# FFT mixing and a routed two-layer network: the transform's steps at other places of a block, outputs scaled a block later, four PSUM banks for the small blocks' second layer

## The chip, the core and the metric

The kernel runs on one core of a Trainium2 chip, as one program. The core's engines work side by side, each through its own queue in order: TensorE (PE: matmuls, with PEld for its weight loads), VectorE (DVE), ScalarE (ACT), GpSimd (POOL, which here also issues the row scatters) and SyncE (SP, which issues most loads and stores). Matmul results land in the banks of PSUM, from where VectorE and ScalarE read them. Semaphores hold an instruction back until what it needs is done.

The metric is the device time of one execution in microseconds. Before the change it is 1346.84, the median of 17 runs (1344.0 to 1351.41).

## The reference

```python
def _attn_ref(x):                      # x: 8 x 2496 x 256
    X = np.fft.fft(x, axis=1)
    X = np.fft.fft(X, axis=2)
    return X.real.astype(np.float32)

def _moe_ref(x, w_gate, w1, w2):       # x: 19968 x 256, 8 experts, F = 1024
    logits = x @ w_gate
    expert_idx = np.argmax(logits, axis=1)
    ...                                # probs: softmax of the logits
    gate_w = probs[np.arange(N), expert_idx]
    ...                                # rows sorted by expert; for expert e:
        h = np.maximum(x_sorted[lo:hi] @ w1[e], 0.0)
        y_sorted[lo:hi] = h @ w2[e]
    ...                                # rows back in place
    return (gate_w[:, None] * y).astype(np.float32)
```

Each of 8 batches of 2496 rows goes through a two-dimensional Fourier transform, of which the real part is kept; each resulting row goes to the one expert with the highest logit, through two matrix products with a ReLU between them, and is scaled by its softmax weight.

## The kernel before

**The transform** of a batch has two stages. `first(b)` folds the input on VectorE (L296 to L308), multiplies it on TensorE (`s`), and stores the result to DRAM as `Td` (L344); `regroup` (L353) loads it back in another order as `t`. `second(b)` (L363) rotates one column (`turn_last`: product `pr`, copy L374), multiplies groups (`group`: product `p` from `t`, copied to `zz` at L381), and for each of ten windows forms output rows and logits (product `p` from `zz`; copy L407; L410, L412; mirrored halves L386). After each five windows `route` (L418) finds the expert of each row by a chain of small VectorE operations (L426 to L433), counts rows before it by matmuls (`rk`), and fixes each row's place (L452 to L457). `send` (L464) then scatters 128 rows at a time into `Xs`, which holds the rows sorted by expert: ScalarE casts the places (`pi`, L469), GpSimd issues the scatter (L237).

**The plan.** When a batch is routed, `plan` (L478) decides which expert's rows each block of the next round takes: some 20 small VectorE operations, at whose end the table `p_tab` stands (L510, L511). SP reads the table into a register and loads a block's rows (`xb`, L530) and its expert's weights (`w1` at L537, `w2` at L539, 1 MB each). `fetch_some` (L783) does so up to three blocks ahead, in SP's queue order; rows only once all scatters of their batch are sent, and weights only once their table is made.

**The blocks.** Each round runs the blocks whose rows are there: rounds of batches 3 to 6 have five blocks of 512 rows, and the last has five of 512, seven of 256 and 21 of 128. A block's rows are transposed (`turn`: product `pt`, copy to `xT` at L579). From batch 3 on a 512-row block, and in the last round a 256-row block too, is computed with seven products in place of eight in each layer (Strassen's scheme in Winograd's form): sums of parts of the operands are formed first. The left operand's sums of layer one are made from w1 by `Left` (L544, VectorE, four steps at L558, into `ws`), during the block before. The right-hand sums come from `xT` (`right`, L563 to L566, VectorE). Layer one is `seven` (L608): 14 products into banks a, d, b, c, e, with sums on VectorE (L629) and copies and ReLUs on ScalarE (L694, L632). Bank b is used by two products, so the second waits until the first was read. Sums of the second layer's left operand stand between the layers: `ends` (L842, L843), `s2` (L890), `s4` (L894), on VectorE; its right operand's sums are `Below` (L588, L601), on GpSimd for 512-row blocks. Layer two is `lower` (L702): seven products into banks a, b and c, with sums into `y` (L726), scaling by the gate (`scaled`, L722, ScalarE) and the scatter of rows to the output (`send_rows`, GpSimd, L237).

**The order** is written out by hand. `experts` is a generator that yields after each product with a weight and a flag. The main loop (from L1014) runs it, and each yield whose flag is not `full` adds to `due`; for each whole unit of `due` one step of `side` is issued (L1030 to L1033). `side` for round b is `mixed(b)` (L954): stage two and routing of batch b woven with stage one of batch b + 1, then the plan. Scatters are issued by their own counter (`room`, L1037). So one engine's queue holds the instructions of the blocks and those of the transform in this written order, and an instruction that waits holds all behind it on its engine.

```python
            if not full:
                due += TICKS * w / ((SHARE if b >= LATE else EARLY) * open_) if w else 1
            while due >= 1:
                next(side, None)
```

## Time and profile before

| What | Value |
|---|---|
| median of 17 runs | 1346.84 us (1344.0 to 1351.41) |
| the profiled execution | 1346.9 us; its span, first to last instruction, 1345.1 us |
| mean granted clock of TensorE | 0.967 |
| busy: PE, DVE, ACT, POOL | 1254.8, 729.5, 504.6, 477.1 us |
| the chain that ended last | PE 77%, DVE 10%, issue 5%, DMA 4%, ACT 2%, POOL 2% |
| w1 and w2 loads, 1024 KB | 132, median 8.0 us from issue to landing |
| row scatters into Xs | 160, mean 1.04 us on POOL |

Rows of the profile name the line, the engine, the operation, and the tiles it writes and reads (out<-in). "x8" counts instructions; a bracket tells how long the engine stood idle before it and what ended this. Each 128x128 block of a matmul in fp32 appears as two records. Line numbers are those of the kernel the profile is of. Rounds of five 512-row blocks run from 346 to 990 us; before this the blocks are of other sizes and use eight products, and behind it the last round runs with no transform beside it.

### The profile page before, as it was taken

To read this page: it belongs to the slowest core of one execution; us is meant where nothing else is said; L and a number is where in the kernel's file an instruction comes from. 1 tells how busy PE (TensorE), PEld (TensorE's weight loads), DVE (VectorE), ACT (ScalarE), POOL (GpSimd) and SP (SyncE) were. 2 spreads that over 40 slices of the span, in tenths; PEclk is the share of its full clock that TensorE was granted. 3 is DMA by queue.
4 is the path that set the end of the run, shared out by engine and by line. 5 is a ranking of instruction groups with operands and counts; after the bars stand their busy time and mean duration, and the time that the engine had idled before them with its cause. 6 is when DMAs were issued, how large, how long until landed. Compare 5 with 4: busy or idle time off the path is not lost.

```text
span 1345.1 us, 23036 instructions
## 1 busy us (share of the span) xinstructions
PE 1254.8 (93%) x8191; PEld 1130.4 (84%) x8191; DVE 729.5 (54%) x1762; ACT 504.6 (38%) x1263; POOL 477.1 (35%) x435
## 2 busy tenths in 40 slices
PE   5769998999989999899999999999999999999997
PEld 3658987776889899898988989888989999999995
DVE  4643242242675756676666755677565663334451
ACT  1423242242345444454444434444433432222232
POOL 0336125034235633276333733275452421111112
PEclk7869999999999999999998999999999999999998
DMA  8877958437335523474332632243432347767675
GB/s 248 255 267 267 395 182 275 144 117 268 122 136 189 198 107 124 143 259 152 123 109 81 229 121 97 97 156 117 170 133 95 103 149 287 253 260 263 246 274 217
DMA packets 63119, 249.88 MB, mean 186 GB/s; under 512 B 10057, under 2 KB 24883, under 8 KB 43420
## 3 DMA queue, kind: packets, MB, share of 16 engines
q1 hardware_dynamic: 46231, 203.33, 43.7%
q0 software_dynamic: 15888, 42.14, 8.6%
q10 hardware_dynamic: 885, 2.94, 0.7%
q8 instruction: 66, 1.08, 0.3%
q14 instruction: 49, 0.40, 0.1%
HBM read 194.97 MB, written 54.83 MB: 186 GB/s over the span
## 4 chain that ended last, share of the span: by engine, by line
PE 77%; DVE 10%; issue 5%; DMA 4%; ACT 2%; POOL 2%; POOLq 0%; SPq 0%; DVEq 0%; ACTq 0%
PE a L222 20%; PE py L222 11%; PE c L222 11%; PE ph L222 11%; PE d L222 5%; PE b L222 5%; PE p L222 5%; PE e L222 3%; PE s L222 3%; PE pt L578 2%; DVE s L842 2%; DVE hT L843 1%; DMA xq<-in_x_dram 1%; DMA Td<-t 1%; DVE hT L629 1%
## 5 line engine op out<-in xcount | busy, mean ns | idle before, releaser
L237 POOL DMA_INDIRECT out_dram<-y,ro x163 | 165.1, 1013 | 600.6 <-ACT y L722 352.1
L237 POOL DMA_INDIRECT Xs<-rows,pi x160 | 166.9, 1043 | 257.4 <-ACT pi L469 155.4
L222 PE MATMUL ph<-xT,w_sb 128*128 128x128 f32 (+2 forms) x992 | 171.3, 329 | 0.8 <-ACT xT L579 0.8
L222 PE MATMUL py<-w_sb,hT 128*128 128x256 f32 x736 | 167.3, 382 | 0.0
L222 PEld LDWEIGHTS ph<-xT,w_sb 128*128 128x128 f32 x992 | 136.5, 193 | 24.8 <-issue 17.0
L222 PEld LDWEIGHTS py<-w_sb,hT 128*128 128x128 f32 x736 | 138.3, 192 | 17.7
L222 PE MATMUL a<-w_sb,hT 128*128 128x128 f32 x912 | 114.7, 278 | 3.3 <-ACT y L747 2.9
L222 PEld LDWEIGHTS a<-w_sb,hT 128*128 128x128 f32 x912 | 109.0, 192 | 10.1 <-ACT y L747 8.6
L859 DVE TENSOR_SCALAR hT<-ph 128x512 f32<-128x512 f32 x43 | 29.7, 690 | 159.9 <-PE ph L222 159.6
L632 ACT ACTIVATE hT<-hT 128x512 f32<-128x512 f32 x114 | 71.7, 631 | 93.3 <-DVE hT L629 93.1
L726 DVE TENSOR_TENSOR y<-y,c 128x256 f32<-128x256 f32 (+1 forms) x64 | 25.1, 392 | 139.9 <-ACT y L747 93.2
L579 ACT ACTIVATE xT<-pt,table 128x512 f32<-128x512 f32 (+1 forms) x94 | 59.2, 630 | 100.2 <-PE pt L578 98.4
L222 PE MATMUL a<-ws,hT 128*128 128x128 f32 x456 | 64.5, 299 | 11.0 <-DVE hT L890 10.9
L629 DVE TENSOR_TENSOR hT<-hT,c 128x512 f32<-128x512 f32 x57 | 39.2, 687 | 62.1 <-PE c L222 49.2
L911 ACT ACTIVATE y<-py,xb 128x256 f32<-128x256 f32 x49 | 23.2, 473 | 131.6 <-PE py L222 127.9
L222 PE MATMUL s<-xq,w 104*112 104x256 f32 (+2 forms) x208 | 61.2, 418 | 11.7 <-DVE xq L299 11.2
L601 POOL TENSOR_TENSOR ws<-w_sb,ws 128x512 f32<-128x512 f32 x50 | 70.7, 1413 | 2.8
L222 PEld LDWEIGHTS a<-ws,hT 128*128 128x128 f32 x456 | 59.9, 209 | 14.0 <-issue 10.4
L578 PE MATMUL pt<-table,xb 128*128 128x128 f32 x326 | 52.6, 278 | 15.6 <-DMA xb<-Xs 15.5
L722 ACT ACTIVATE y<-y,xb 128x128 f32<-128x128 f32 (+1 forms) x114 | 46.4, 449 | 51.8 <-DVE y L726 51.8
L410 DVE COPY lg<-p 128x16 f32<-128x16 f32 x80 | 13.8, 172 | 93.2 <-ACT zs L407 93.1
L222 PE MATMUL p<-table,t 120*128 120x120 f32 (+1 forms) x352 | 58.7, 293 | 4.9 <-ACT t L374 4.1
(162 smaller groups left out, 2570.2 us busy)
## 6 DMA issues: line engine op xcount, KB each, us to landing
w_sb<-in_moe_w_dram SPq DMA_DIRECT2D x132, 1024.0 KB, 8.0
xq<-in_x_dram SPq DMA_DIRECT2D x24, 896.0 KB, 9.0
xb<-Xs SPq DMA_DIRECT2D x28, 516.0 KB, 3.9
Td<-t SPq DMA_DIRECT2D x18, 448.0 KB, 3.3
t<-Td SPq DMA_DIRECT2D x8, 768.0 KB, 12.2
t<-Td SPq DMA_DIRECT2D x8, 640.0 KB, 13.9
xb<-Xs SPq DMA_DIRECT2D x13, 258.0 KB, 3.2
xb<-Xs SPq DMA_DIRECT2D x25, 129.0 KB, 3.3
```

The source lines that it names most:

```text
L222: nc.tensor.matmul(o, lhsT=lhsT, rhs=rhs, start=start, stop=stop, **kw)
L237: return unordered(pool.indirect_dma_start(out=dst, out_offset=bass.IndirectOffsetOnAxis(ap=idx, axis=0), in_=rows, in_offset=None, bounds ...
L578: nc.tensor.transpose(pt[:, c, t], xb[:, 2 * h + t, c * 128:(c + 1) * 128], ident[:])
L579: act.activation(xT[:, :, 256 * h:256 * h + 128 * n], pt[:].rearrange("p c t k -> p c (t k)"), ACTF.Copy, scale=con["alt"][:])
L601: self.eng.tensor_tensor(o, p, q, op=sub)
L629: vec.tensor_tensor(o, o, p[:], op=add)
L632: act.activation(o, o if p is None else p[:], ACTF.Relu)
L722: act.activation(y[k][:, i, lo:hi], y[k][:, i, lo:hi] if src is None else src[:, i], ACTF.Copy, scale=gate[:, k * nt + i])
L726: vec.tensor_tensor(o, o, p[:], op=add)
L842: vec.scalar_tensor_tensor(s1[:, at], h21[:, at], 0.0, h11[:, at], op0=ALU.max, op1=add)
L859: vec.tensor_scalar(o, ph[:], 0.0, None, op0=ALU.max)
L911: act.activation(y[:, i % 2], py[:], ACTF.Copy, scale=xb[:, i, D + 1:D + 2])
```

## The change

The yields of `seven` and `lower` now carry a second flag, so that steps of the transform are issued at three products of layer one (4 and 6) and behind the last four products of layer two only, and not between the layers' sums. Those of layer two weigh 1 and 4/3. A step of the transform may yield True (after the last window but one of the first half, and twice in routing); then no other step is issued at that place. `SHARE` goes from 0.6 to 0.9 and the open weight per block from 8 to 6.5, so the steps of a round are spread over more of it.

In `seven`, the sums of a half (`ends`) stand behind its last addition, and the weight sums (`step`) at other products. In `lower` for 512 rows the product 6 comes ahead of 5 and the transposes later; the second half of the output is scaled and sent by `rest`, which runs in the next block's layer one, ahead of the fourth of GpSimd's sums. For 256 rows `lower` is written anew with bank d, and in another order of products. The copy of the transposes moves from ScalarE to VectorE, but for the 512-row blocks with seven products. The number of matmuls stays the same.

```diff
--- before.py
+++ after.py
@@ -184,7 +184,7 @@
 
 TICKS = 32
 LATE = 4
-SHARE, EARLY, ROOM = 0.6, 0.7, 1.2
+SHARE, EARLY, ROOM = 0.9, 0.7, 1.2
 WARM = 16
 MOST = max(k for now in rounds() for _, k, _ in now)
 
@@ -411,7 +411,7 @@
                 for m, op in enumerate((ALU.add, ALU.subtract)):
                     vec.scalar_tensor_tensor(rows[:, k + m, 0:NY], p3[:, 0:NY], zs[:, 0:1], zs[:, 1:],
                                              op0=ALU.add, op1=op)
-                yield
+                yield w + 2 == HALF - 1
             mirror(rows, k)
             yield from route(b, h, rows, lg)
 
...
@@ -576,8 +576,11 @@
             for c in range(2):
                 for t in range(n):
                     nc.tensor.transpose(pt[:, c, t], xb[:, 2 * h + t, c * 128:(c + 1) * 128], ident[:])
-            act.activation(xT[:, :, 256 * h:256 * h + 128 * n], pt[:].rearrange("p c t k -> p c (t k)"), ACTF.Copy,
-                           scale=con["alt"][:])
+            o, i = xT[:, :, 256 * h:256 * h + 128 * n], pt[:].rearrange("p c t k -> p c (t k)")
+            if size == BIG and quartered(b, size):
+                act.activation(o, i, ACTF.Copy, scale=con["alt"][:])
+            else:
+                vec.tensor_scalar(o, i, con["alt"][:], None, op0=ALU.mult)
             yield xT
         if halved(b, size):
             th = size // 2
...
         a, b, c = [bank("a"), bank("d")], [None, None], [None, None]
         for k, g in ((0, 0), (0, 1), (1, 0), (5, 0), (5, 1), (1, 1), (4, 0), (4, 1), (6, 0), (6, 1), (2, 0), (3, 0),
@@ -684,22 +687,27 @@
                 product(g, 3, c[g], False)
                 plus(h21[g], c[g])
                 low(g)
-                if g:
-                    ends(0)
+                ends(g)
             else:
                 product(g, k, a[g], not k)
                 if k == 2:
                     relu(h12[g], a[g])
                 else:
                     act.copy({0: h11, 5: h21, 4: h22}[k][g], a[g][:])
-            if k in (0, 5):
+            if k == 0 or (k, g) in ((1, 1), (4, 0)):
                 step()
-            else:
+            if (k, g) == (4, 1):
+                step()
+                for f in later:
+                    f()
+                later.clear()
+            if k not in (0, 5):
                 sums()
-            yield
-        ends(1)
-
-    def lower(size, l, r, y, gate, send_rows, turn_some, s2, s4):
+            yield 4 <= k <= 6 and (k, g) not in ((5, 0), (5, 1), (6, 1))
+
+    later = []
+
+    def lower(size, l, r, y, gate, send_rows, turn_some, s2, s4, step):
 
 
 
@@ -726,38 +734,83 @@
             vec.tensor_tensor(o, o, p[:], op=add)
 
         a, b, c = (bank(k) for k in "abc")
+        if nt == 1:
+            d = bank("d")
+            p1, u2, u3 = y[1][:, 0:nt, 0:H], y[1][:, 0:nt, H:], y[0][:, 0:nt, 0:H]
+            high = y[0][:, 0:nt, H:]
+            product(0, a)
+            act.copy(p1, a[:])
+            s2()
+            turn_some()
+            yield False
+            product(3, b)
+            yield False
+            product(1, a, False)
+            s4()
+            step()
+            turn_some()
+            yield False
+            product(5, c)
+            vec.tensor_tensor(u2, p1, c[:], op=add)
+            scaled(1, 0, H, a)
+            yield False
+            product(6, d)
+            vec.tensor_tensor(u3, u2, d[:], op=add)
+            step()
+            turn_some()
+            yield False
+            c = bank("c")
+            product(4, c)
+            vec.tensor_tensor(high, u3, c[:], op=add)
+            plus(u3, b)
+            plus(u2, c)
+            scaled(0, 0, D)
+            send_rows(0)
+            step()
+            yield False
+            d = bank("d")
+            product(2, d)
+            plus(u2, d)
+            scaled(1, H, D)
+            send_rows(1)
+            step()
+            yield False
+            return
         p1, u2, v = y[1][:, 0:nt, 0:H], y[0][:, 0:nt, 0:H], y[0][:, 0:nt, H:]
         product(0, a)
         act.copy(p1, a[:])
         s2()
-        yield
+        yield False
         product(1, b)
         s4()
         plus(p1, b)
-        yield
-        turn_some()
-        yield
+        yield False
+        product(6, c)
+        yield False
         product(5, a, False)
         act.copy(u2, a[:])
         scaled(1, 0, H)
-        yield
-        product(6, c)
-        yield
+        turn_some()
+        yield 1
         product(4, a, False)
         act.copy(v, a[:])
         plus(v, c)
         turn_some()
-        yield
+        yield 4 / 3
         product(2, a, False)
         scaled(1, H, D, a)
         send_rows(1)
         turn_some()
-        yield
+        yield 4 / 3
         product(3, c, False)
         plus(u2, c)
-        scaled(0, 0, D)
-        send_rows(0)
-        yield
+
+        def rest():
+            scaled(0, 0, D)
+            send_rows(0)
+
+        later.append(rest)
+        yield 4 / 3
 
     def experts(todo):
 
@@ -797,6 +850,10 @@
 
         for k, (b, size, last, at) in enumerate(todo):
             n, m = size // 128, BIG // size
+            if not (size == BIG and halved(b, size)):
+                for f in later:
+                    f()
+                later.clear()
             if not k:
                 while todo[0][:3] not in tabs:
                     yield 0, False
@@ -843,10 +900,10 @@
                     vec.scalar_tensor_tensor(h21[:, at], h21[:, at], 0.0, h22[:, at], op0=ALU.max, op1=sub)
 
             if halved(b, size):
-                for _ in seven(size, left.all, xT, hT, both, sums, step, ends):
+                for open_ in seven(size, left.all, xT, hT, both, sums, step, ends):
                     if size != BIG:
                         sums()
-                    yield 0.5, True
+                    yield 0.5, not open_
             for f in range(0 if halved(b, size) else FC // m):
                 ph = pse.tile([128, m, size], F32, tag="ac"[f % 2], name="ph")
                 with needed(last, at, ph):
@@ -876,7 +933,7 @@
             if both:
                 y = [bp.tile([128, 2, D], F32, tag="y", name="y", bufs=3) for _ in range(2)]
 
-                def send_rows(k):
+                def send_rows(k, n=n, ro=ro, y=y):
                     for i in range(n // 2):
                         at = k * n // 2 + i
                         put_row(out, ro[:, at:at + 1], y[k][:, i], NT - 1, "out")
@@ -895,9 +952,10 @@
 
                 while below.due:
                     below.step()
-                for _ in lower(size, (h22, h12, h12, h11, s1, h22, h21), below.all, y, xb[:, :, D + 1:D + 2],
-                               send_rows, turn_some, s2, s4):
-                    yield 1, False
+                for open_ in lower(size, (h22, h12, h12, h11, s1, h22, h21), below.all, y, xb[:, :, D + 1:D + 2],
+                                   send_rows, turn_some, s2, s4,
+                                   left.step if follow and halved(*follow[:2]) else lambda: None):
+                    yield open_ or 1, not open_
             for i in range(0 if both else n):
                 xT = next(turned, xT)
                 py = pse.tile([128, D], F32, tag="bd"[i % 2], name="py")
...
@@ -929,10 +989,11 @@
         parts = list(parts)
         while parts:
             for p in list(parts):
-                if next(p, p) is p:
+                r = next(p, p)
+                if r is p:
                     parts.remove(p)
                 else:
-                    yield
+                    yield r
 
     def close(b):
 
@@ -957,10 +1018,10 @@
         for _ in range(3):
             next(one, None)
             yield
-        for k, _ in enumerate(two):
+        for k, r in enumerate(two):
             if k % 2:
                 next(one, None)
-            yield
+            yield r
         yield from woven(close(b), one)
         yield from through(b)
 
@@ -1018,7 +1079,7 @@
             side = woven(chain(close(0), through(0)), chain(early, side))
         blocks = [(size, k * size / BIG, halved(b - 1, size)) for size, k, _ in rounds()[b - 1]]
         total = sum(k * (15 if seven_ else 16) for _, k, seven_ in blocks)
-        open_ = sum(k * (8 if seven_ else 16) for _, k, seven_ in blocks)
+        open_ = sum(k * (6.5 if seven_ else 16) for _, k, seven_ in blocks)
         while done < total:
             w, full = next(work)
             done += w
@@ -1029,8 +1090,9 @@
                 whole.update(p[0] for p in tabs if p != "cnt")
             if not full:
                 due += TICKS * w / ((SHARE if b >= LATE else EARLY) * open_) if w else 1
-            while due >= 1:
-                next(side, None)
+            stay = False
+            while due >= 1 and not stay:
+                stay = next(side, None) and halved(b - 1, BIG)
                 due -= 1
                 if b < LATE or not w:
                     send()
```

The cut places hold the two `yield True` of `route`, the seven `yield False` of the small form of `seven`, and the last run of what waits in `later` at the end.

More of the change, by code (lines that the diff above doesn't have):

```diff
@@ L433, in route @@
         vec.tensor_tensor(oh[:, 0:NSL], bc(con["rev"][:], 1, NSL), bc(v[:], 2, E), op=ALU.is_equal)
-        yield
+        yield True
         su = small("su", NSL)
@@ L439, in route @@
         vec.tensor_scalar(rows[:, :, D], con["row"][:, h], float(b * S), None, op0=ALU.add)
-        yield
+        yield True
         rk = pm_.tile([128, NSL + 1, E], F32, tag="m", name="rk")
@@ L728, in lower @@
         a, b, c = (bank(k) for k in "abc")
+        if nt == 1:
[17 more added lines that the diff above has]
+            scaled(1, 0, H, a)
+            yield False
+            product(6, d)
+            vec.tensor_tensor(u3, u2, d[:], op=add)
+            step()
+            turn_some()
+            yield False
+            c = bank("c")
[6 more added lines that the diff above has]
+            step()
+            yield False
+            d = bank("d")
[4 more added lines that the diff above has]
+            step()
+            yield False
+            return
         p1, u2, v = y[1][:, 0:nt, 0:H], y[0][:, 0:nt, 0:H], y[0][:, 0:nt, H:]
@@ L732, in lower @@
         s2()
-        yield
+        yield False
         product(1, b)
@@ L736, in lower @@
         plus(p1, b)
-        yield
-        turn_some()
-        yield
+        yield False
+        product(6, c)
+        yield False
         product(5, a, False)
@@ L742, in lower @@
         scaled(1, 0, H)
-        yield
-        product(6, c)
-        yield
+        turn_some()
+        yield 1
         product(4, a, False)
@@ L749, in lower @@
         turn_some()
-        yield
+        yield 4 / 3
         product(2, a, False)
@@ L754, in lower @@
         turn_some()
-        yield
+        yield 4 / 3
         product(3, c, False)
         plus(u2, c)
-        scaled(0, 0, D)
-        send_rows(0)
-        yield
+        def rest():
[3 more added lines that the diff above has]
+        yield 4 / 3
     def experts(todo):
@@ L918, in experts @@
                     left.step()
+        for f in later:
+            f()
     def pads(b):
@@ L931, in woven @@
             for p in list(parts):
-                if next(p, p) is p:
+                r = next(p, p)
+                if r is p:
                     parts.remove(p)
                 else:
-                    yield
+                    yield r
     def close(b):
@@ L959, in mixed @@
             yield
-        for k, _ in enumerate(two):
+        for k, r in enumerate(two):
             if k % 2:
                 next(one, None)
-            yield
+            yield r
         yield from woven(close(b), one)
```

## The prediction

> **What bounds the kernel now.** The page first: how busy each engine is, and the clock.
>
> ```profile
> PE 1254.8 (93%) x8191; PEld 1130.4 (84%) x8191; DVE 729.5 (54%) x1762; ACT 504.6 (38%) x1263; POOL 477.1 (35%) x435
> ...
> PEclk7869999999999999999998999999999999999998
> ```
>
> TensorE is the bound. Both programs hold the same 4511 matmuls, so only TensorE's idle time and its half-clock stretches can change. Its view of waits says who ends the idle time:
>
> ```profile
> PE pt L578 <- DMA xb<-Xs: 15.5, 4, 7.1
> PE rk L222 <- DVE oh L433: 15.5, 6, 3.0
> ...
> PE a L222 <- DVE hT L890: 10.9, 12, 3.1
> ...
> PE p L222 <- ACT t L374: 4.1, 4, 1.1
> PE b L222 <- ACT hT L632: 3.8, 7, 0.5
> ...
> PE a L222 <- ACT y L747: 2.9, 8, 0.5
> PE b L222 <- DVE hT L629: 2.3, 4, 0.6
> ```
>
> (Columns: microseconds in total, times, longest.) By time, four rounds of five 512-row blocks (346 to 990 us) hold these: per round one rk wait of 3.03 (2.55 in the fourth), one wait of 1.6 for the sums (L890), one of 1.1 for the rotation (L374), one of 0.57 (L629). The timeline shows the longest:
>
> ```profile
> 399.47 1.29 DVE L894 TENSOR_TENSOR hT<-hT 128x512 f32<-128x512 f32 x2
> 400.67 0.42 DVE L726 TENSOR_TENSOR y<-y,b 128x256 f32<-128x256 f32 x1
> 401.01 0.23 DVE L426 TENSOR_REDUCE mx<-lg 128x10 f32<-128x80 f32 x1
> ...
> 402.29 0.24 DVE L433 TENSOR_TENSOR oh<-table,v 128x80 bf16<-128x80 f32 x1
> ...
> 402.59 0.21 PE L222 MATMUL rk<-oh,tri 128*128 128x88 bf16 x1 [3.03 <-DVE oh L433]
> ```
>
> Routing's eight small operations stand in VectorE's queue behind the sums (L894), and rk behind them. A long gap also costs clock. Of the windows view the last three columns are read, the granted clock, the DMA share and GB/s:
>
> ```profile
> 226.20:231.50 5.30, 0.25 (x2) 0.00 (x0) 0.69 (x1) 0.00 (x0) 0.59 (x1) 0.84 0.49 155
> 231.50:236.30 4.80, 4.54 (x13) 3.83 (x14) 0.17 (x1) 0.69 (x1) 0.00 (x0) 0.50 0.98 338
> ...
> 402.30:407.00 4.70, 4.41 (x34) 4.41 (x35) 3.08 (x14) 2.44 (x7) 0.00 (x0) 0.66 0.00 0
> ```
>
> After a gap of 5.3 us the clock is 0.50 for 4.8 us, so 2.4 us lost; after 3.03 us it is 0.66 over 4.7 us, so 1.6 lost. After the gaps of 1.6 it stays 1.00.
>
> **The change, part by part.** Sums are against the profiled execution: 1346.9 us (span 1345.1 and 1.8 around it); the median of the 17 runs is 1346.84, so no correction.
>
> *Routing off the sums.* In the changed order rk stands after the first product of layer one of the third block. I walk VectorE from the last table product before it: TensorE needs one layer-two product (1.80, starts 366.39 to 368.19), a stage-one pair (0.86) and one layer-one product (0.86, starts 380.39, 381.25), 3.5 in all; VectorE has the rest of the right-hand sums, logits and rows (1.5), four folds (1.7) and the routing chain (1.5), ready at 4.7. So a wait of 1.2 stays: 11.6 becomes 4.8, **-6.8**, and 4 x 1.6 of clock, **-6.4**. But folds and the first two weight sums (L558) then queue ahead of L629, on which the product into bank b waits: 0.57 grows to 1.7 by the same walk, **+4.5** (bounds: 0 more, and 2 more each). The second routing has a whole layer to finish: no wait.
>
> *Sums earlier, product six ahead of product five.* The L890 wait of four blocks (1.59, 1.58, 1.57, 1.32) and 0.5 of the 3.1 at the last planning: **-6.6**. The other 2.6 stays, since two plans (4.4 us of VectorE each) still stand there. Rotation and its use are now in different gaps: **-4.1**. Two more waits of the fourth round (L726 1.46, L694 1.78): half, **-1.6**.
>
> *256-row blocks.* 1.15 us of small gaps in each of seven blocks (b 0.55, a 0.35 and 0.25) and 0.4 before the first; with four banks only the second sums' finish is left, 0.2 each: **-6.6**.
>
> *Moved at no cost.* Scaling the second half of the output a block later puts two scalings (0.50 each) on ScalarE and two row stores (1.28 apart) on GpSimd into the next block's layer one; ScalarE is busy 45% there. The next block's first copy waits for these stores to land; they land 1.5 us before it is due, and its own reader is 5 us away: 0, up to +1 where GpSimd is late. The transform's own loads and stores (Td, t, xq on SP) move with their steps; the last, t, leaves in the fourth block, over 25 us ahead of the round that reads it: 0. The transposes' copies of early and small blocks go from ScalarE (0.69) to VectorE (0.69 for a like shape), both with idle time there: 0, within 1 of either sign.
>
> Gains: 6.8 + 6.4 + 6.6 + 4.1 + 1.6 + 6.6 - 4.5 = **27.6**.
>
> *The pace.* This is where I look for the loss. Before, 32 / (0.6 x 8 x 5) = 1.33 steps fall on each of 8 places of a block, 10.7 per block; after, 32 / (0.9 x 6.5 x 5) on 6.5, 7.1 per block. The 26 steps of a round end in the fourth block, not in the third, and the plan of the next round is its end. Its table is the last thing VectorE makes before the fifth block. In the changed order SP's load of w1 for the next round's first block stands right at the start of the fifth block, and VectorE's queue has the first L558 of that very load directly after the plan, ahead of both L629 that free bank b. Before, a whole block (26 us) lay between. Rows for the price:
>
> ```profile
> 445.21 0.16 DVE L511 TENSOR_SCALAR p_tab<-p_ei 1x21 int32<-1x21 f32 x1
> ...
> 446.17 0.36 SPq L537 DMA_DIRECT2D w_sb<-in_moe_w_dram  x1
> ...
> 1121.75 0.34 SPq L537 DMA_DIRECT2D w_sb<-in_moe_w_dram  x1
> ...
> 1127.68 0.69 DVE L558 TENSOR_TENSOR ws<-w_sb 128x512 f32<-128x512 f32 x1 [3.21 <-DMA w_sb<-in_moe_w_dram]
> ```
>
> From the table's end to the load 0.8; from load to L558 5.9 in the tail; the page's median landing of these loads is 8.0. I take 6.5, since SP issues little else then. With the fifth block's first product at 0: table done +0.25 (its chain starts from the second half of xT, copied at -2.6, then 1.7 of right-hand sums and 1.0 of plan), load +1.05, landed +7.55, two L558 (1.4) and one L629 (0.7): bank b free at +9.7. Its product, the sixth, is due at 5 x 0.86 = 4.3. **A wait of 5.4 us** (4.8 by the tail's row, 6.9 by the median), in each of four rounds: +21.6. The clock after it, by the 5.3 us row, 2.4 each: +9.6.
>
> GpSimd comes next. The batch's last scatters slip a block too, and the next block's xb is loaded when the last has landed. ScalarE's index casts stand behind its ReLU, which waits for the same L629. So: ReLU, copy, cast done at 11.2; one scatter, two sums (1.3 each); the cast for the next scatter 14.2; the stores of the last block's rows after their scaling at 16.4 and 17.7 (1.28 apart); a sum until 20.0; four scatters, the last starting at 24.1. Layer two starts at 9.7 + 9 x 0.86 + 2.4 = 19.9, so this is 4.2 into it.
>
> ```profile
> 465.68 1.09 POOL L237 DMA_INDIRECT Xs<-rows,pi  x1 [0.30 <-issue]
> 468.55 0.34 SPq L530 DMA_DIRECT2D xb<-Xs  x1
> ...
> 327.94 1.56 SPq L530 DMA_DIRECT2D xb<-Xs  x2
> ...
> 331.57 0.66 PE L578 MATMUL pt<-table,xb 128*128 128x128 f32 x4 [1.58 <-DMA xb<-Xs]
> ```
>
> Last scatter to load 2.9, load to transposes 3.6: the rows are there 10.7 into layer two. The transposes are due after four products, at 7.2. I take **3.5 us** (bounds 0 and 5) per round, +14.0, and 1.6 of clock by the rk row, +6.4.
>
> Losses: 21.6 + 9.6 + 14.0 + 6.4 = **51.6**. Sum: 1346.9 - 27.6 + 51.6 = **1370.9**; I say 1371.
>
> *A page against the row.* TensorE: Matmul & The Clock Gate, of the Trainium skill, section "HAM oscillation — how this bites in real kernels", tells one to keep TensorE's gaps under about 3.4 us, as the clock then falls to a half; that speaks against this change, which turns gaps of 3 into gaps of over 5. The trace shows half clock already behind 3.03 us. With its one busy window of 3.4 us at half, as an estimate, the loss behind each long gap would be 1.7 in place of 2.4, and the sum 2.8 lower.
>
> **The rivals.**
> *Faster: the rows arrive in time.* If the last scatter starts within 0.7 us of the fifth block's layer two (7.2 - 3.6 - 2.9), the xb wait and its clock vanish; with the load at the tail's 5.9 (a wait of 4.8) and 1.6 of clock a round loses 6.4, under the 6.9 (27.6 / 4) at which it is even: 1346.9 - 27.6 + 25.6 = 1344.9, and 1340 with rk's rest of 4.8 hidden. For it: before, the batch's last scatters started 17.5 us after a block's start, 5.4 into layer two, and there was no wait behind the table then: against it.
> *Slower still: routing's wait only moves.* If rk and bank b's product wait as long as rk did, 13.2 of the gain is gone and 4.5 more lost at most: 1384 to 1389. For it: VectorE has 9 us of work in the 10 around the start of the third block.
> *The late loads repeat.* The second weight load of the new round is issued behind xb; if it lands after its block's start, L558 waits again, up to 3 us in four rounds: 1382. It lands about 1 us ahead by my walk.
>
> **How the numbers follow.** Chances: main case 0.62, faster rival 0.13, moved wait 0.13, repeated load 0.12. About 0.2% (2.7 us) is what a measurement of this kernel tells from no change. The faster rival lies partly within that: 0.10 faster and 0.03 the same; with 0.01 from the main case's low end, faster 0.11, same 0.03, slower 0.86. The main case alone: losses of 4 x (4.8 + 1.6 + 1.5) = 32 to 4 x (6.9 + 2.4 + 5 + 1.6) = 64 and gains of 22 to 34 make 1345 to 1389 at its corners. The range, 1346 to 1391, leaves out the faster rival and a little above.
>
> **What would show it.** In the profile after: waits of VectorE at L558 for w1, four of 4 us or more, between the first and the last 512-row round, and TensorE's longest waits being b on DVE (bank b) there, at about 5 us, four times; pt on xb four times more than now; rk's total near 9 (from 15.5); L890's near 4; the waits of b on L632 (3.8) gone. The prediction is wrong if the L558 rows show no wait for the load in these rounds, or if its gap is not passed on to TensorE; then the gains stand alone, near 1320.

## The result and the profile after

The changed kernel takes 1378.8 us (median of 8 runs, 1376.2 to 1381.4), the kernel before 1347.7 (47 runs). The ratio is 1.0234, with a 95% interval of 1.0219 to 1.025: slower. Its profiled execution took 1382.7 us, with a span of 1380.9. From here on line numbers of the changed kernel's family are its own: the addition into a bank's sums, L629 before, is L632; the copies into hT, L694, are L696; s2, L890, is L947; ends, L842 and L843, are L899 and L900; the ReLU, L632 before, is L635.

The page of the changed kernel, busy time and granted clock:

```profile
PE 1269.9 (92%) x8191; PEld 1138.2 (82%) x8191; DVE 775.9 (56%) x1827; ACT 476.3 (34%) x1205; POOL 477.9 (35%) x435
...
PEclk6779999999999999999899999999999999999998
```

With the same matmuls TensorE is busy 15 us longer, which fits the half clock in the table, and the span is 36 longer. The trace gives each stage. "Half clock" in the table is half of the time in which the granted clock was 0.50 and TensorE not idle; in the last stage it and the idle time are counted up to TensorE's last matmul.

| stage, us | before: length, idle, half clock | after: length, idle, half clock |
|---|---|---|
| to the first round of 512-row blocks with seven products | 346.1, 41.8, 20.3 | 346.6, 41.7, 21.0 |
| the four rounds | 617.8, 28.0, 7.9 | 663.9, 55.4, 24.1 |
| the last 512-row blocks, then 256 and 128 rows | 376.4, 13.4, 2.7 | 364.8, 6.7, 0.2 |

The four rounds lose 46.1 us: 27.4 more idle and 16.2 more at half clock. The last stage gains 11.6. TensorE's waits in the changed kernel (total us, times, longest) name what ends the idle time:

```profile
PE pt L578 <- DMA xb<-Xs: 30.9, 8, 7.2
PE b L222 <- DVE hT L632: 22.1, 10, 4.4
PE rk L222 <- DVE oh L433: 13.4, 7, 3.1
...
PE c L222 <- DVE hT L632: 4.7, 4, 1.4
...
PE c L222 <- POOL w_sb L604: 3.1, 1, 3.1
PE a L222 <- DVE hT L947: 2.1, 1, 2.1
```

The waits for xb are twice those of before, bank b's went from 6.1 to 22.1, and rk's hardly fell (from 15.5). The waits for the rotation (L374), and of b and a in the 256-row blocks, are gone, but for one of a of 0.5. The timeline of the fifth block of the first round shows the new wait whole:

```profile
475.86 0.45 DVE L511 TENSOR_SCALAR p_tab<-p_ei 1x21 int32<-1x21 f32 x1
...
477.08 0.37 SPq L537 DMA_DIRECT2D w_sb<-in_moe_w_dram  x1
...
482.72 0.69 DVE L558 TENSOR_TENSOR ws<-w_sb 128x512 f32<-128x512 f32 x1 [5.60 <-DMA w_sb<-in_moe_w_dram]
483.44 0.69 DVE L558 TENSOR_TENSOR ws<-ws,w_sb 128x512 f32<-128x512 f32 x1
484.05 0.68 DVE L632 TENSOR_TENSOR hT<-hT,b 128x512 f32<-128x512 f32 x1
...
484.79 1.13 PE L222 MATMUL b<-xT,w_sb 128*128 128x256 f32 x4 [4.03 <-DVE hT L632]
```

From the table to the load 0.8 us, from the load to the L558 that waited for it 5.6, then two L558 and one L632, and bank b is free. L558 waits 5.60, 5.53, 5.58 and 3.64 us in the four rounds, bank b's product 4.03, 3.96, 4.01 and 4.45. This is the prediction's main step. What it had not seen is how rk's wait came to stay:

```profile
576.57 1.41 POOL L604 TENSOR_TENSOR ws<-w_sb 128x512 f32<-128x512 f32 x1
576.77 0.23 DVE L426 TENSOR_REDUCE mx<-lg 128x10 f32<-128x80 f32 x1
577.04 1.04 DVE L427 TENSOR_TENSOR eq<-lg,mx 128x80 f32<-128x80 f32 x1
578.06 2.60 POOL L604 TENSOR_TENSOR ws<-w_sb,ws 128x512 f32<-128x512 f32 x2
578.12 1.30 DVE L428 TENSOR_TENSOR eq<-eq,table 128x80 f32<-128x80 f32 x1
579.45 0.24 DVE L429 TENSOR_REDUCE v<-eq 128x10 f32<-128x80 f32 x1
579.73 0.96 DVE L430 TENSOR_TENSOR v<-v,table 128x10 f32<-128x10 f32 x1
...
580.72 0.24 DVE L433 TENSOR_TENSOR oh<-table,v 128x80 bf16<-128x80 f32 x1
...
581.02 0.21 PE L222 MATMUL rk<-oh,tri 128*128 128x88 bf16 x1 [3.07 <-DVE oh L433]
```

The same operations in the kernel before, with no sum of GpSimd beside them:

```profile
401.27 0.24 DVE L427 TENSOR_TENSOR eq<-lg,mx 128x80 f32<-128x80 f32 x1
401.55 0.24 DVE L428 TENSOR_TENSOR eq<-eq,table 128x80 f32<-128x80 f32 x1
...
402.09 0.17 DVE L430 TENSOR_TENSOR v<-v,table 128x10 f32<-128x10 f32 x1
```

Routing's operations L427, L428 and L430 took 0.24, 0.24 and 0.17 us before; in the changed kernel's rows above 1.04, 1.30 and 0.96, and each ends 0.1 us or less behind the end of one of GpSimd's sums (L604). The two reductions beside the same sums take 0.23 and 0.24, as ever. The chain from L426 to L433 took 1.53 us in each first routing before, and now 3.15, 4.19, 4.19 and 2.69.

### The profile page after: what moved, and what is told of

It reads as the page before. It is cut to its first block, busy times and chain, and to the rows that moved or that the text cites. A ratio compares the mean times of both kernels' runs of the same rounds, so it can differ in the third digit from the quotient of the medians.

```text
span 1380.9 us, 23027 instructions
## 1 busy us (share of the span) xinstructions
PE 1269.9 (92%) x8191; PEld 1138.2 (82%) x8191; DVE 775.9 (56%) x1827; ACT 476.3 (34%) x1205; POOL 477.9 (35%) x435
## 5 line engine op out<-in xcount | busy, mean ns | idle before, releaser
L635 ACT ACTIVATE hT<-hT 128x512 f32<-128x512 f32 x114 | 71.4, 630 | 115.5 <-DVE hT L632 115.4
L222 PE MATMUL b<-xT,w_sb 128*128 128x256 f32 x200 | 57.0, 411 | 22.1 <-DVE hT L632 22.1
L222 PE MATMUL s<-xq,w 104*112 104x256 f32 (+2 forms) x208 | 61.4, 419 | 13.0 <-DVE xq L299 11.6
L604 POOL TENSOR_TENSOR ws<-w_sb,ws 128x512 f32<-128x512 f32 x50 | 71.8, 1436 | 3.3
L578 PEld LDWEIGHTS pt<-table,xb 128*128 128x128 f32 x326 | 41.2, 149 | 34.7 <-issue 17.8
L222 PEld LDWEIGHTS b<-xT,w_sb 128*128 128x128 f32 x200 | 39.7, 203 | 31.7 <-DVE hT L632 26.1
L632 DVE TENSOR_TENSOR hT<-hT,b 128x512 f32<-128x512 f32 x50 | 34.2, 684 | 53.0 <-PE b L222 39.9
L918 ACT ACTIVATE hT<-ph 128x512 f32<-128x512 f32 x55 | 32.8, 597 | 89.2 <-PE ph L222 86.8
L222 PE MATMUL p<-table,zz 128*128 128x145 f32 (+1 forms) x320 | 57.1, 303 | 4.5 <-DVE rows L412 3.5
```

The lines of the kernel that those rows point to most:

```text
L222: nc.tensor.matmul(o, lhsT=lhsT, rhs=rhs, start=start, stop=stop, **kw)
L578: nc.tensor.transpose(pt[:, c, t], xb[:, 2 * h + t, c * 128:(c + 1) * 128], ident[:])
L604: self.eng.tensor_tensor(o, p, q, op=sub)
L632: vec.tensor_tensor(o, o, p[:], op=add)
L635: act.activation(o, o if p is None else p[:], ACTF.Relu)
L918: act.activation(o, ph[:], ACTF.Relu)
```

## The experiments

Theory L: the loss is the late plan (w1 and the last scatters come late). Theory G: VectorE's operations are held up by GpSimd's sums that lie beside them. Rival theory P: the places themselves fill VectorE's queue. One table for all runs; the middle columns are from each run's trace, over the four rounds and the last stage. In the group of e7_memset, e8_share08, e9_share075 and e2_before09 the kernel before itself took 1370.5 us, some 23 more than in the others. The first stages of these four runs are 13 to 19 us longer, which is not all of it, so the ratios are to be compared; between the groups, times of the rounds compare only roughly.

| run | ratio to before, 95% | rounds: length, idle, half clock | last stage |
|---|---|---|---|
| before | 1 | 617.8, 28.0, 7.9 | 376.4 |
| after | 1.0234 (1.0219 to 1.025) | 663.9, 55.4, 24.1 | 364.8 |
| e1_share06 | 1.008 (1.0049 to 1.011) | 636.4, 36.4, 12.7 | 366.9 |
| e5_share085 | 1.000 (0.9974 to 1.0026) | 628.3, 31.9, 7.1 | 366.9 |
| e3_left_late | 1.0293 (1.0248 to 1.0338) | 658.8, 59.1, 11.1 | 373.1 |
| e4_room08 | 1.0281 (1.0245 to 1.0317) | 667.6, 60.3, 23.0 | 364.6 |
| e7_memset | 0.9869 (0.9834 to 0.9904) | 628.3, 32.0, 14.8 | 362.2 |
| e8_share08 | 1.0182 (1.016 to 1.0205) | 658.8, 53.1, 15.0 | 368.3 |
| e9_share075 | 0.9926 (0.9905 to 0.9948) | 626.0, 28.2, 6.0 | 366.1 |
| e2_before09 | 1.0082 (1.0065 to 1.0099) | 637.5, 40.7, 13.4 | 379.1 |
| e10_w_first | 1.0026 (1.0015 to 1.0037) | 630.3, 32.0, 9.5 | 368.8 |
| e6_lower256 | 0.9924 (0.9908 to 0.9939) | 618.4, 28.7, 7.9 | 366.5 |
| e11_mixed | 0.9928 (0.9915 to 0.9941) | 622.2, 25.6, 6.7 | 365.3 |
| e12_undo_moved | 1.0291 (1.0272 to 1.0311) | 661.6, 57.1, 19.1 | 368.0 |

**The pace put back.**

```diff
-SHARE, EARLY, ROOM = 0.9, 0.7, 1.2
+SHARE, EARLY, ROOM = 0.6, 0.7, 1.2
```

> The changed kernel with SHARE put back to 0.6: the steps of a round end in the third block (table made behind product 2 of its layer two), all else as changed. Theory, that the late plan is what costs: VectorE's waits at L558 between the rounds go (4 of 3.6 to 5.6 us), and with them TensorE's waits for bank b (16.5 us in four) and for xb (14.6 us in three), and the half clock behind them (some 16 us). From 1378.8 that leaves about 1332, and 1320 to 1345 if routing's wait (11.6 us) changes too, as rk then stands five products behind its one-hot rows. Rival, that the fewer places are what costs: with the old pace on 6.5 places, 1.6 steps instead of 1.3 fall on a place, VectorE's queue is fuller at each, and new waits take the place of the old; 1360 or more.

1354.98 us: between the two. L's waits go as expected: between the rounds L558 does not wait, nor do xb and rk, and of bank b one wait is left (5.1, in the fourth round). But 22.0 us of waits for bank e in 11 places are new. The timeline at one of them:

```profile
435.39 1.86 DVE L492 TENSOR_TENSOR p_lo<-bt,p_nb 1x64 f32<-1x64 f32 x1
435.88 1.29 POOL L604 TENSOR_TENSOR w_sb<-w_sb 128x512 f32<-128x512 f32 x1
...
437.61 0.68 DVE L632 TENSOR_TENSOR hT<-hT,e 128x512 f32<-128x512 f32 x1
...
438.35 1.07 PE L222 MATMUL e<-xs,w_sb 128*128 128x256 f32 x2 [3.56 <-DVE hT L632]
```

Operations of routing and of the plan stand ahead of L632 now, and one of them, of 64 numbers on one partition, takes 1.86 us beside a sum of GpSimd. So L is right on what goes, and P on what comes; neither alone gives the time.

**The pace put back a little.**

```diff
-SHARE, EARLY, ROOM = 0.9, 0.7, 1.2
+SHARE, EARLY, ROOM = 0.85, 0.7, 1.2
```

> The changed kernel with SHARE 0.85: the table of the next round is finished one product of layer two (1.8 us) earlier, and the last scatter is issued behind the second product of the fifth block's layer one instead of the second of its layer two, some 14 us earlier. Theory of the late plan: L558's waits for w1 shrink by 1.8 us each, bank b's waits from 4.0 to about 2.2 (-7), the xb waits (14.6 us in three) go with their clock (some 6), so 1348 to 1358. Rival, that the load itself is slow at this place, whenever it is issued: L558's waits stay at 4 or more and only the xb part goes, 1358 to 1365.

1346.72 us, ratio 1.000: all of the loss is gone with one step of the pace, a little below what was expected. L558's waits are 3.80, 4.06 and 3.70 where they were 5.60, 5.53 and 5.58: 1.5 to 1.9 shorter, near the 1.8 of the theory. But bank b's waits, 3.4, 5.0, 2.0 and 4.9, did not follow. The second of them:

```profile
629.63 0.37 SPq L537 DMA_DIRECT2D w_sb<-in_moe_w_dram  x1
...
635.98 2.39 DVE L558 TENSOR_TENSOR ws<-w_sb 128x512 f32<-128x512 f32 x1 [4.06 <-DMA w_sb<-in_moe_w_dram]
636.53 1.28 POOL L604 TENSOR_TENSOR ws<-w_sb 128x512 f32<-128x512 f32 x1
637.89 3.28 POOL L604 TENSOR_TENSOR ws<-w_sb,ws 128x512 f32<-128x512 f32 x2
638.41 1.63 DVE L558 TENSOR_TENSOR ws<-ws,w_sb 128x512 f32<-128x512 f32 x1
...
640.69 1.65 PE L222 MATMUL b<-xT,w_sb 128*128 128x256 f32 x3 [5.00 <-DVE hT L632]
```

The two L558 took 2.39 and 1.63 us beside GpSimd's sums, 0.69 each without. What paid was elsewhere: xb's waits went, and rk's too, since routing's chain took 1.53 us in all four rounds; with them went 17 us of half clock.

**The weight sums moved.**

```diff
-            if k == 0 or (k, g) in ((1, 1), (4, 0)):
+            if (k, g) in ((6, 0), (6, 1), (2, 0), (3, 0)):
                 step()
             if (k, g) == (4, 1):
-                step()
                 for f in later:
```

> The changed kernel with the four weight sums at L558 moved from products (0,0), (0,1), (1,1), (4,0) of a 512-row block's layer one to (6,0), (6,1), (2,0), (3,0); the plan stays as late as it is. Theory, that bank b waits only because the L558 that waits for w1 stands ahead of L632 in VectorE's queue: L558 itself waits 0 to 2 us, bank b's four waits of 4.0 to 4.5 go with their clock (about 10), the xb waits stay: 1350 to 1360. Rival, that bank b waits for VectorE's backlog of plan and folds and L558 only lies in it: three or more us of bank b's wait stay, 1370 or more. A cost of either: 2.8 us of VectorE more at the end of layer one, up to 1 us a block at the start of layer two.

1384.25 us: in time this is the rival's (1370 or more), but the waits are those of the theory. What was asked is answered: L558 waits no more between the rounds and bank b's waits are gone (0.4 in all), so they came from the L558 that waits ahead of L632. But the four sums now delay ends at the end of layer one: c waits for ends 16.0 us in 15 places, in the last stage too, e for L632 14.5 in 11, and xb's waits rose to 5.9, 6.5 and 6.0. The cost put at "up to 1 us a block" was up to 1.2 for c and up to 1.7 for e in most blocks.

**The scatters closer together.**

```diff
-SHARE, EARLY, ROOM = 0.9, 0.7, 1.2
+SHARE, EARLY, ROOM = 0.9, 0.7, 0.8
```

> The changed kernel with ROOM 0.8 instead of 1.2, so that scatters follow each other more closely: the batch's last is issued behind the eighth product of the fifth block's layer one, not behind the second product of its layer two (about 7 us earlier). The table stays late. Theory, that the xb waits come from late scatters alone: these three waits (4.5, 4.55, 5.6) go with their half clock, bank b's waits stay at 4.0 to 4.5: 1378.8 - 14.6 - 6 = 1358 (1355 to 1365). Rival, that the scatters are held up by GpSimd's weight sums or by ScalarE's casts and not by the place at which they are issued: the xb waits stay at 3 us or more each, 1370 to 1380.

1382.54 us: no gain, and above both ranges. xb's waits fell from 4.5, 4.55 and 5.6 to 1.7, 1.75 and 2.6, so they came from late scatters for the greater part. But a wait of bank d came, 2.83 us in three rounds and 4.0 in the fourth, and bank b's rose to 5.2:

```profile
445.99 1.93 DVE L427 TENSOR_TENSOR eq<-lg,mx 128x80 f32<-128x80 f32 x1
...
446.52 1.29 POOL L604 TENSOR_TENSOR ws<-w_sb 128x512 f32<-128x512 f32 x1
447.89 2.61 POOL L604 TENSOR_TENSOR ws<-w_sb,ws 128x512 f32<-128x512 f32 x2
...
451.66 0.27 ACT L438 ACTIVATE lg<-lg 128x80 f32<-128x80 f32 x1 [4.82 <-DVE lg L437]
...
452.95 1.42 PE L222 MATMUL d<-xs,ws 128*128 128x256 f32 x3 [2.83 <-ACT hT L696]
```

With the scatters earlier, GpSimd reached its sums where the second routing runs: that chain took 5.1 us here, ScalarE's exponential waited for it, and bank d's copy stood behind the exponential in ScalarE's queue.

**GpSimd's sums without reads.**

```diff
-                self.eng.tensor_tensor(o, p, q, op=sub)
+                if self.eng is pool:
+                    pool.memset(o, 0.0)
+                else:
+                    self.eng.tensor_tensor(o, p, q, op=sub)
```

> The changed kernel with GpSimd's four sums of w2 in each 512-row block replaced by memsets of the same tiles, which read nothing; this leaves the second layer's right-hand sums out of the computation. Theory, that routing is late because its operations with two SBUF inputs wait for GpSimd's sums (the chain from L426 to L433 took 3.15, 4.19, 4.19 and 2.69 us in the third block, beside such sums, and 1.5 alone): the chain takes 1.5 everywhere, rk's waits of 2.04, 3.07, 3.07 and 1.10 fall by what the chain gets shorter, to 0.5, 0.4, 0.4 and 0, and the half clock behind them goes: about 8 us of waits and 5 of clock, so 1360 to 1368. GpSimd gets freer by up to 5 us a block too, so the xb waits may fall as well, to 1350 at the lowest. Rival, that the queue ahead of routing is simply longer than was walked (copies, folds): the chain gets shorter by less than 0.5 or rk's waits stay at 2 to 3 us; 1373 or more. Bank b's waits for the late load stay at 4.0 to 4.5 in either case.

Ratio 0.9869, far below the expectation (1360 to 1368 was 1.010 to 1.016): G is right in its place and was priced too low. In the same place as above:

```profile
584.89 1.49 POOL L605 MEMSET ws<- 128x512 f32 x3
585.12 0.23 DVE L426 TENSOR_REDUCE mx<-lg 128x10 f32<-128x80 f32 x1
585.38 0.24 DVE L427 TENSOR_TENSOR eq<-lg,mx 128x80 f32<-128x80 f32 x1
585.66 0.24 DVE L428 TENSOR_TENSOR eq<-eq,table 128x80 f32<-128x80 f32 x1
...
586.71 0.21 PE L222 MATMUL rk<-oh,tri 128*128 128x88 bf16 x1 [0.42 <-DVE oh L433]
```

Beside GpSimd's memsets the chain takes 1.53 to 1.59 us; rk waits 0.47, 0.42, 0.41 and less. Bank b's waits of the second block (1.4) and the c waits of the fourth (1.38) are gone as well, bank b's four in the fifth block stay (4.0, 4.1, 4.1, 3.8), as do L558's (5.6, 5.7, 5.6, 3.0): that part is L's. The memsets also take 0.5 us each in place of 1.3, so GpSimd is freer; xb's waits fell to 3.6, 2.1 and 3.9. By the ratios (1.0234 and 0.9869) the memsets are worth 49 us, by the rounds of the two traces 35.6. How much of it is that freedom and how much the reads, this run does not part.

**Two more steps of the pace.** The first of them failed:

```diff
-SHARE, EARLY, ROOM = 0.9, 0.7, 1.2
+SHARE, EARLY, ROOM = 0.8, 0.7, 1.2
```

> The changed kernel with SHARE 0.8: the table is finished two products of layer two (3.6 us) earlier than at 0.9, one earlier than at 0.85. Theory of the late plan: L558's waits for w1, 5.5 at 0.9 and 3.8 at 0.85, are 2.0 here; bank b's waits fall by 1.8 against 0.85; 1335 to 1343. Rival, as with SHARE 0.6: the denser steps bring new waits of bank e and c for L632; 1347 to 1355.

Ratio 1.0182: against both expectations. L558 waits 8.3, 6.4 and 8.4 us, though the table is earlier. The timeline, of the scatters, SP's loads and L558:

```profile
486.00 0.44 DVE L511 TENSOR_SCALAR p_tab<-p_ei 1x21 int32<-1x21 f32 x1
490.02 0.97 POOL L237 DMA_INDIRECT Xs<-rows,pi  x1 [3.59 <-ACT pi L469]
492.98 0.37 SPq L530 DMA_DIRECT2D xb<-Xs  x1
...
494.41 0.10 SPq L537 DMA_DIRECT2D w_sb<-in_moe_w_dram  x1
...
501.65 0.69 DVE L558 TENSOR_TENSOR ws<-w_sb 128x512 f32<-128x512 f32 x1 [8.30 <-DMA w_sb<-in_moe_w_dram]
```

At this pace the batch's last scatter is issued before the fifth block begins, so fetch_some writes the load of xb, and w1 behind it, into SP's queue. SP waits there for that scatter (5.6 us in its own view of waits), and w1 leaves 8 us behind its table.

```diff
-SHARE, EARLY, ROOM = 0.9, 0.7, 1.2
+SHARE, EARLY, ROOM = 0.75, 0.7, 1.2
```

> The changed kernel with SHARE 0.75: the table is finished three products of layer two (5.4 us) earlier than at 0.9. Theory of the late plan: L558 does not wait for w1 any more (0.2 or less), bank b's four waits go, 1325 to 1338. Rival, as with SHARE 0.6: the denser steps bring new waits of bank e and c for L632; 1345 to 1355.

Ratio 0.9926, 0.7% faster than before. No L558 waits between the rounds, as L expected. Rounds one to three are at 155.4, 155.6 and 154.6 us; the fourth stays at 160.3, with 5.4 of bank b behind its two plans. The expected 1325 to 1338 would have been 0.984 to 0.994: inside, at its end, as c waits of 1.8 to 2.3 in the fourth block came in.

**The weights ahead of the rows**, in fetch_some, at SHARE 0.8:

```diff
                 n = len(xbs)
+                b, size, last, at = todo[k + len(got)]
+                if size == BIG and halved(b, size) and len(got) <= n and (b, size, last) in tabs:
+                    got.append(fetch_weights(tabs[b, size, last], at))
                 b, size, last, at = todo[k + n]
...
                 elif n < len(got):
                     break
+                if len(got) > n:
+                    continue
```

> The changed kernel with SHARE 0.8, and for the 512-row blocks with seven products fetch_some issues a block's weights ahead of its rows. With SHARE 0.8 alone the ratio to the kernel before was 1.018 and L558 waited 8.3, 6.4 and 8.4 us, longer than at 0.9, though the table was earlier: w1 was issued 8 us behind the table, right behind the load of xb. Theory, that w1 stood in SP's queue behind the load of xb, which waits there for the last scatter: now w1 is issued 0.8 us behind the table, L558 waits under 1 us, bank b's waits in the fifth block fall from 6.6, 4.7 and 6.6 to under 2, and the ratio to 0.999 to 1.008. Rival, that two loads beside each other are slow, whichever is first: L558 still waits 3 us or more, 1.012 or more.

Ratio 1.0026, as the theory expected. The same place:

```profile
472.60 0.44 DVE L511 TENSOR_SCALAR p_tab<-p_ei 1x21 int32<-1x21 f32 x1
473.80 0.37 SPq L537 DMA_DIRECT2D w_sb<-in_moe_w_dram  x1
...
476.63 0.97 POOL L237 DMA_INDIRECT Xs<-rows,pi  x1 [3.59 <-ACT pi L469]
479.86 0.68 DVE L558 TENSOR_TENSOR ws<-w_sb 128x512 f32<-128x512 f32 x1
...
483.49 0.34 SPq L530 DMA_DIRECT2D xb<-Xs  x1
```

w1 leaves 0.8 us behind the table, ahead of the scatter that held it, and L558 waits no more. The price of that queue, SHARE 0.8 with and without this edit, is 21 us by the ratios (1.0182 and 1.0026); the rounds of the two traces, which are of different groups, differ by 28.

**The kernel before at the new pace.**

```diff
-SHARE, EARLY, ROOM = 0.6, 0.7, 1.2
+SHARE, EARLY, ROOM = 0.9, 0.7, 1.2
```

> The kernel before with SHARE 0.9 and nothing else changed: its pace becomes that of the changed kernel, 7.1 steps a block; the table comes behind the last product of the fourth block, the last scatter at product (3,0) of the fifth, and the first routing's rk behind the last product of layer two. Theory, that the late plan costs by itself, whatever the places: L558 waits 4 to 5.5 us for w1 in four rounds, the product into bank b waits some 4 us behind it (+16) with 2 of clock each (+8), against rk's wait that partly goes with its new place (-4 to -14): 1347 to 1367, and the L558 and bank-b waits are in the profile. Rival, that it costs only together with the new places: no L558 waits over 2 us between the rounds, and 1335 to 1347.

Ratio 1.0082, inside the theory's 1.000 to 1.015, but made of other parts than expected: L558 waits 2.2, 2.9, 2.1 and 1.1 us and bank b behind it 1.5 at most, while xb's waits, 5.4, 4.8, 5.6 and 5.6, make most of the loss, and bank b of the second block waits 3.4, 2.2 and 2.2 in three rounds (0.6 before); rk's waits are gone. So the late plan costs by itself, through the rows more than through w1.

**The 256-row blocks alone**: the kernel before with the new branch of lower for nt == 1 (as in the diff of the change) and nothing else.

> The kernel before with one part of the change alone: the new layer two of the 256-row blocks, with its four banks and its order of products. Theory, that this part is independent of the others and worth the small gaps before these blocks' products (a on y 2.9 us and b on L632 3.8 us in the waits of before): 5 to 11 us faster, ratio 0.992 to 0.996. Rival, that the shorter last stage of the changed kernel (365 us from the last round's first block to the end, against 376) came from the 512-row blocks in it: 0.998 to 1.001.

1336.29 us, ratio 0.9924. The waits of TensorE in the last stage of this run, from 964 us on:

```profile
PE a L222 <- DVE hT L932: 3.1, 1, 3.1
PE pt L578 <- DMA xb<-Xs: 2.2, 1, 2.2
PE a L222 <- ACT y L789: 0.5, 1, 0.5
```

Of the waits shown before, b on L632 (3.8) is gone and a on y (2.9) is down to one of 0.5. The rounds are as before (618.4). The last stage is 9.9 us shorter, 6.7 of it idle time; some 3.5 lie in no gap and no half clock, and stay unexplained.

**A mixed pace.**

```diff
-SHARE, EARLY, ROOM = 0.9, 0.7, 1.2
+SHARE, EARLY, ROOM = 0.75, 0.7, 1.2
...
             if (k, g) == (4, 1):
                 step()
-                for f in later:
-                    f()
-                later.clear()
             if k not in (0, 5):
                 sums()
+            if (k, g) == (4, 1):
+                for f in later:
+                    f()
+                later.clear()
...
-                due += TICKS * w / ((SHARE if b >= LATE else EARLY) * open_) if w else 1
+                due += TICKS * w / (((SHARE if b < B - 1 else 0.6) if b >= LATE else EARLY) * open_) if w else 1
```

> The changed kernel with SHARE 0.75 (ratio 0.9926 to the kernel before), but 0.6 for the last round with a transform, and the rows of the block before sent behind GpSimd's fourth sum, not ahead of it. Theory: the fourth round loses its wait of 5.4 us for bank b behind the two plans or at least its clock (3 to 5 us less), and the one wait of 3.1 us for the fourth sum (L604) goes with 1 to 2 of clock: 0.986 to 0.990. Rival, that both only move on to the next wait: 0.991 to 0.995.

Ratio 0.9928: the rival's. The wait for the fourth sum is gone (0.65 on a sum of VectorE in its place), so with this order of GpSimd's queue the row stores ahead of the sum held it up. But the fourth round stays at 161.1: waits of 3.7 for bank e and 5.1 for bank b. On the same chip the new 256-row layer alone has 0.9924: at the best pace tried, the other parts of the change together are worth nothing that could be measured.

**The parts costed at nothing, undone.**

```diff
-        later.append(rest)
+        rest()
...
-            if size == BIG and quartered(b, size):
+            if True:
                 act.activation(o, i, ACTF.Copy, scale=con["alt"][:])
```

> The changed kernel with the two parts undone that the prediction costed at nothing: the second half of the output is scaled and sent at the block's end again, and all copies of the transposes are on ScalarE again. By the prediction nothing changes: 1.020 to 1.026, the ratio of the changed kernel being 1.0234; of the changed kernel's waits only the single one of 3.1 us for GpSimd's fourth sum goes, since the row stores no longer stand ahead of it. Rivals: the later scaling is what loads the start of the blocks, and without it 0.5 to 1 us a block comes back, 1.005 to 1.015; or it had cleared the block's end, and its undoing costs as much, 1.030 or more.

Ratio 1.0291, slightly slower than the changed kernel (1.0234) and just under the second rival; the two profiled executions stand the other way (1379.9 and 1382.7), so the size stays open. What the trace shows is that these parts were not neutral. With the rows sent at the block's end, GpSimd's sums fall elsewhere: routing's chain takes 1.53 to 1.59 us, rk waits 0.47 at most, but bank b in the second block now waits 3.98, 3.99 and 3.98 us (1.4 in the changed kernel), behind a fold (L297, L298: 2.42 and 1.75 us, 0.68 alone) and an L558 (1.64) beside the same sums. The wait for the fourth sum was expected to go, and 2.6 of its 3.1 us stayed, so the later place of the row stores had made 0.5 of it at most.

## Why the prediction was right, and where not

1371 was predicted, 1378.8 measured, inside the range, on the predicted side and by the predicted mechanism. Against the profiled execution (1382.7) the sum is 12 short. By its terms, as predicted and as the trace has them:

| term | predicted | measured |
|---|---|---|
| rk's wait, four rounds | -6.8 | -2.3 (11.6 to 9.3) |
| bank b, second block | +4.5 | +2.2 (2.3 to 4.5) |
| the sums' wait | -6.6 | -7.1 (9.2 to 2.1) |
| the rotation's wait | -4.1 | -4.1 |
| two waits of the fourth round | -1.6 | -3.2 |
| 256-row blocks | -6.6 | -10.7 alone (1347.0 to 1336.3) |
| bank b behind the late load | +21.6 | +16.4 |
| xb late | +14.0 | +14.6, in three rounds |
| half clock in the rounds | +9.6 | +16.2 |
| c on L632, three of 1.38; c on L604, 3.1 | none | +7.2 |

Terms that came out dearer than predicted (18.9 us together) and cheaper (13.7) partly cancel, so that the sum came this near is in part luck. By these terms the change costs 29.2 us, and the two profiled executions lie 35.8 apart; the rest is in none of them.

*The late plan.* Right, step by step: table to load 0.8 as walked, load to L558 5.6 where 6.5 was taken, so 4.0 to 4.45 of bank b and not 5.4. The moved weight sums show that L558 is the link, SHARE 0.85 that its wait follows the table, and 0.8 with its mended order that SP's queue decides when w1 leaves. The prediction gave bounds for the load's time and took its place in SP's queue for granted; at SHARE 0.8 that place was worth more, 8 us, where the load takes 5.6.

*xb.* 3.5 us in each of four rounds was walked; it was 4.5, 4.55 and 5.6 in three. In the fourth there was none, as TensorE itself came later, held by bank b (4.45) and by the sums (2.1), behind two plans.

*Routing: the step that failed.* The prediction put "the routing chain (1.5), ready at 4.7. So a wait of 1.2 stays". The order was right, the chain's duration not: 3.15, 4.19, 4.19 and 2.69, as GpSimd's sums lie beside it, and rk waits 2.04, 3.07, 3.07 and 1.10. The row for 1.5 came from a place without such sums. So the gain of 6.8 was 2.3, and its 6.4 of clock did not come: half clock still follows three of the four. The runs show the cause from two sides: with memsets, or where the sums lie elsewhere, the chain takes 1.5 and rk waits 0.5 at most. The c waits of 1.38 and bank b's 1.4 go with the memsets too.

*Moved at no cost.* The copies and the scaling were costed at nothing "within 1"; the runs show that the place of GpSimd's sums depends on them, and with it which product waits: rk with the change, bank b of the second block without them. In time their undoing made the kernel slightly slower (1.0291 against 1.0234). Of the single wait for the fourth sum (3.1) 2.6 stayed without the later row stores.

*The rivals.* The faster one (rows in time) is what SHARE 0.85 made real: no wait for xb, at 1346.7 where it said 1344.9; but rk's wait went too, and bank b's waits did not fall, so the nearness of the number is partly luck. "Routing's wait only moves" came true by half, by a cause that it did not name. The second weight load of the round did not come late.

The rule of the Trainium skill that would have found the failed step stands in the page SBUF — State Buffer, section "Who interferes with whom": "A DVE instruction with two SBUF inputs contends with a GpSimd instruction that reads SBUF", and the sentence goes on "not with one that only writes it". This case's rows agree. In the changed kernel's rounds L558 in place in w1 (two inputs in SBUF) takes 0.68 us alone and 2.38 beside L604 in the median, while L632 (one input in PSUM) takes 0.69 both times. Beside memsets L558 takes 0.68 or 0.69 too.

## What to carry to other kernels

Walk an engine's queue with the durations that its operations have in their new place: where GpSimd reads SBUF beside them, VectorE's operations with two SBUF inputs last until GpSimd's end, and a small chain on the critical path can then cost one such sum for each of these operations. When a producer is moved later, look at what is written into the same queue as its consumer's load: a load that waits for one thing holds all loads behind it, so an earlier table gave a later weight. Take a change of many parts apart by parts: here the gain sat in one part, the 256-row blocks, and the pace decided over the rest.

## What the runs showed of the hardware

- VectorE beside GpSimd's sums of 1.3 us: fold L298 0.68 alone and 1.75 beside, a copy of 8 numbers a partition (L299) 0.17 and 1.23, a product on one partition (L492, in e1_share06) 0.2 and 1.86; reductions and operations with an input in PSUM are not held up. Small held operations end 0.1 us or less behind the end of a sum, whatever their own length; L298 ends 0.54 behind it. In the changed kernel the sums get longer as well, up to 1.8 us.
- Beside memsets the operations with two SBUF inputs are not held up (L427 0.24, L558 0.68), but some with one are: L439 took 0.64 and 1.06 us in e7_memset, 0.17 alone.
- In the rounds half clock came in stretches of 3.4 or 6.8 us, in the changed kernel behind all gaps of TensorE of 2.0 us and more between 340 and 1010 us, from 2.04 on, and behind none of 1.44 and less; behind a gap of 3.09 at 1030 us it did not come. In the other runs some gaps of 2.0 to 3.1 stayed without, every gap of 3.4 or more had one, and three times it came behind two short gaps close together (1.18 and 0.68 us in e8_share08, 1.45 and 0.64 in e3_left_late, 1.60 and 0.44 in e11_mixed). The page TensorE: Matmul & The Clock Gate of the Trainium skill, section "HAM oscillation — how this bites in real kernels", puts the limit at about 3.4 us; by these runs gaps of 2 to 3 are a risk already.
- A 1 MB load of weights (w1) with no other load issued just ahead of it was used 5.6 us after its issue, with w2's load of 1 MB issued 0.6 us behind it; 7.2 where the load of xb was issued 1.4 us ahead of it.
